# Four edits to a recurrence-and-MLP kernel: u by one row, weight sums on GpSimd, separate PSUM banks at the end, and a reordered list

## The chip, the cores and the metric

One core of a Trainium2 chip. The metric is the device time of one execution in microseconds, the median of several runs. Profiles are of one execution by the hardware profiler; its times count from the first instruction.

## The reference

Two layers run one after the other. First a recurrence over 768 steps for each of 4 sequences and 8 heads of 48 channels, with a state of 48 x 48 per head; then an MLP with the greater of two products over the 3072 tokens of width 384.

```python
for t in range(S):                                  # B, H, S, D = 4, 8, 768, 48
    kt, vt, rt, wt = (k[:, :, t], v[:, :, t], r[:, :, t], w[:, :, t])
    cur = np.einsum('bhd,bhe->bhde', u[None] * kt, vt)
    y[:, :, t] = np.einsum('bhd,bhde->bhe', rt, state + cur)
    state = wt[:, :, :, None] * state + np.einsum('bhd,bhe->bhde', kt, vt)
...
x = y.transpose(0, 2, 1, 3).reshape(B * S, H * D)   # 3072 x 384
out = np.maximum(x @ w1, x @ w2) @ w_out            # d_ff = 1024
```

All inputs and the output are float32.

## The kernel before

**Units.** The 768 steps are cut into 6 chunks of 128, the 4 sequences into 2 pairs. A unit is one chunk of one pair: 12 units, 0 to 11, with units 2c and 2c+1 being chunk c of the two pairs. Inside a unit, index b (0 or 1) is the sequence, and a tile has the 128 steps as its partitions and 8 x 48 = 384 columns.

**The recurrence of a unit** (the names are those of the list that orders the work). ScalarE takes the logarithm of w (lw; from unit 3 on also a rounded copy lwh, and VectorE the rest lwl). TensorE sums the logarithms over the steps by a product with a triangle (ex, L245), VectorE adds the step's own (incl). ScalarE makes exp of the exclusive sum (aex) and exp of minus the inclusive one (ainv), and VectorE multiplies them onto r and k (rp, kp). TensorE transposes both (T), ScalarE copies them out of PSUM (TO, tile rkT), TensorE makes the 128 x 128 products of each head (M), VectorE masks them (MO). TensorE applies them to v and, after the first chunk, adds the carried state (Y). The term with u goes another way: GpSimd multiplies k, u and r (ku L297, rku L302), VectorE sums over the 48 channels (dg), GpSimd multiplies the sum onto v (bv L310), and VectorE adds it to Y (YO). TensorE transposes the result (X), VectorE copies it (XO, tile xT). The state: K on TensorE, sa and sm on VectorE, sb on GpSimd; the chunk's decay goes through DRAM (row L268 writes the last row of incl to DRAM, wt L273 reads it back as columns into Wt, wx on ScalarE takes exp).

**The MLP of a unit.** The greater of h1 and h2 is (h1 + h2)/2 + |h1 - h2|/2. So wd = w1 - w2 and ws = w1 + w2 are built once in bfloat16 (wdif L201, wsum L198, both on VectorE), ws is transposed (wT on TensorE, wTO on ScalarE) and multiplied with w_out into wc (wp L214, 3 x 8 matmuls of 384 columns into PSUM tile wc_p; wpO on ScalarE scales by 0.5). For a unit: H (L410) makes x times wd in four groups f2 of six matmuls of 256 columns, and HO (L422) takes the absolute value on ScalarE into gT; O1 (L430) starts an output sum with three matmuls of x times wc and four of gT times w_out, O2 (L437) adds the other four; OO (L440) copies to osb on ScalarE and st (L445) stores it. O1 and O2 run for each b.

**Loads.** All go out on SP's queue, in the order of the list: ldw, ldr, ldk, ldv (L225), a whole unit (384 KB, in rows of 192 bytes) or one sequence of it (192 KB) at a time; units 0 to 2 are mostly loaded by sequence. ldw12 (L180) loads a third of w1 and of w2 (two DMAs of 512 KB), ldwo (L186) half of w_out (768 KB), which ScalarE casts to bfloat16 (woc L192). Both kinds share the same two buffers ("w12"), in turns: w12.2 takes the buffer of w12.0, wof.0 that of w12.1, wof.1 that of w12.2, when wsum and wdif have read them. u is one DMA that writes its 384 numbers to all 128 partitions (ldu L195).

**PSUM.** Tag "mlp" has two buffers and serves H, O1, wT, wp and the like; tag "ex" has two for ex and ainv.

**Order.** The list ORDER (L17) is written out by hand, and every engine works its share of it strictly in that order. A step stands as name.unit.b, or name.unit.f2 for H and HO. "warm" (L171) issues matmuls of a blank tile that nothing reads: fillers in the first 30 us, 52 in all. TensorE's order near the end of the start is

```
M.1.1 H.0.3 ex.2.0 Y.1.1 X.1.0 X.1.1 ex.2.1 H.1.0 H.1.1 K.1 wp.1 wp.0 wp.2 H.1.2 T.2.0 O1.0.0 ...
```

and ScalarE's is HO.0.2, ..., woc.0, HO.0.3, woc.1, HO.1.0, HO.1.1, aex.2.0, and on.

Of the kernel before, what the change touches and what calls it, by code (L numbers as in the profile page):

```python
# [8 lines left out]
F32 = mybir.dt.float32  # L9
# [20 lines left out]
ainv.2.1 sa.1 kp.2.1 HO.1.2 TO.2.0 ku.2.0 rku.2.0 ku.2.1 rku.2.1 sb.0.0 sb.0.1 O1.0.0 ex.3.0 incl.3.0 dg.2.0  # L30
ex.3.1 M.2.0 incl.3.1 MO.2.0 lw.4 aex.3.0 O2.0.0 O1.0.1 O2.0.1 wx.1 lwh.4 OO.0.0 vb.2.0 aex.3.1 vb.2.1 T.2.1
H.1.3 K.2 OO.0.1 O1.1.0 TO.2.1 lwl.4 sm.1 rp.3.0 dg.2.1 rp.3.1 sa.2 ainv.3.0 ainv.3.1 HO.1.3 M.2.1 Y.2.0
sb.1.0 bv.2.0 ku.3 bv.2.1 rku.3 sb.1.1 ldr.4 ldv.3 wt.2 kp.3.0 kp.3.1 MO.2.1 YO.2.0 T.3.0 TO.3.0 O2.1.0 ex.4.0
ex.4.1 incl.4.0 incl.4.1 M.3.0 Y.2.1 T.3.1 YO.2.1 O1.1.1 MO.3.0 X.2.0 X.2.1 O2.1.1 OO.1.0 lw.5 lwh.5 aex.4.0
TO.3.1 aex.4.1 rp.4.0 XO.2 M.3.1 ainv.4.0 OO.1.1 H.2.0 H.2.1 ldk.4 ldw.6 row.3 ldv.4 ldr.5 wt.3 row.4 ldk.5
vb.3 wx.2 HO.2.0 HO.2.1 K.3 rp.4.1 lwl.5 dg.3 sm.2 ainv.4.1 H.2.2 H.2.3 bv.3 ku.4 rku.4 sb.2.0 sb.2.1 kp.4.0
sa.3 kp.4.1 T.4.0 TO.4.0 HO.2.2 HO.2.3 lw.6 ex.5.0 Y.3.0 ex.5.1 T.4.1 MO.3.1 YO.3.0 M.4.0 Y.3.1 O1.2.0 O2.2.0
incl.5.0 MO.4.0 YO.3.1 incl.5.1 X.3.0 X.3.1 XO.3 TO.4.1 O1.2.1 M.4.1 O2.2.1 vb.4 aex.5.0 OO.2.0 lwh.6 rp.5.0
dg.4 lwl.6 H.3.0 Y.4.0 ainv.5.0 aex.5.1 OO.2.1 kp.5.0 rp.5.1 wx.3 HO.3.0 H.3.1 H.3.2 HO.3.1 HO.3.2 ainv.5.1
ldw.7 row.5 bv.4 sm.3 MO.4.1 kp.5.1 YO.4.0 ku.5 sb.3.0 sb.3.1 rku.5 wt.4 ldr.6 T.5.0 H.3.3 TO.5.0 HO.3.3 wx.4  # L40
lwh.7 lw.7 ex.6.0 O1.3.0 ex.6.1 incl.6.0 incl.6.1 aex.6.0 aex.6.1 Y.4.1 O2.3.0 T.5.1 YO.4.1 X.4.0 X.4.1 M.5.0
# [31 lines left out]
def kernel(  # L73
# [12 lines left out]
    nc = tc.nc  # L86
    B, H, S, D = r.shape
# [408 lines left out]
```

## Time and profile before

| | |
|---|---|
| Median of 7 runs | 160.07 us (159.03, 159.44, 159.66, 160.07, 161.06, 161.53, 161.69) |
| Profiled execution, its own time | 162.65 us |
| Its span, first to last instruction | 160.8 us |
| Busy: PE, PEld, DVE, ACT, POOL | 147.3, 100.7, 118.2, 113.7, 80.2 us |
| Mean granted TensorE clock | 0.988 |
| DMA | 28.82 MB, mean 179 GB/s; 107,802 of 112,822 packets under 512 bytes |

The span is what the profile can explain; the execution's own time is 1.85 us longer. PE is TensorE's matmuls, PEld its weight loads, DVE VectorE, ACT ScalarE, POOL GpSimd, SP the engine that issues the DMAs. A line such as L217 is a line of the kernel printed above. A row of a group gives the operation, its shapes, how often it ran, the busy time and the mean of one. A matmul's own duration overlaps the next one's, so the cost of a group of matmuls is read from the time between its starts (the chain of waits gives that). The chain of waits follows the work that ended last back from the last instruction, at each step to what released it.

### The profile page before, as it was taken

Reading aid. Unit: us, or ns where it says so; the run is one execution under the profiler, and the core shown is the slowest. Engines: PE = TensorE matmul, PEld = TensorE weight load, DVE = VectorE, ACT = ScalarE, POOL = GpSimd, SP = SyncE. Lnnn points to the kernel's source line nnn. Section 1 sums busy time; section 2 is a strip of 40 time slices with the busy share of each in tenths; the row PEclk is TensorE's granted clock in tenths of the full one; section 3 lists DMA queues with packets and bytes.
Section 4 is the critical chain, followed back from the end, with each engine's and each line's share of the span. In section 5 each row is a group of like instructions: output and inputs, shape, how many; then the busy total and the mean of one; then the engine's idle time right before and its main releaser. Section 6 shows DMA issues by size and latency. Waiting matters only on the chain.

```text
span 160.8 us, 3996 instructions
## 1 busy us (share of the span) xinstructions
PE 147.3 (92%) x1588; PEld 100.7 (63%) x1588; DVE 118.2 (73%) x185; ACT 113.7 (71%) x202; POOL 80.2 (50%) x80
## 2 busy tenths in 40 slices
PE   6988868973999999999999999979999999999991
PEld 2434434742476777768787686757786768777760
DVE  3168969871359999999799889995998888942100
ACT  4255247955789798898979889794986977664541
POOL 8274600800390862959508694890775468630000
PEclk9999999999599999999999999999999999999999
DMA  5999996996989899696999779968999994020202
GB/s 103 205 320 197 290 359 135 183 353 125 198 148 231 157 171 226 103 201 121 227 217 169 117 156 233 220 184 151 181 197 223 285 307 177 0 75 27 98 0 98
DMA packets 112822, 28.82 MB, mean 179 GB/s; under 512 B 107802, under 2 KB 112026, under 8 KB 112804
## 3 DMA queue, kind: packets, MB, share of 16 engines
q1 hardware_dynamic: 112804, 28.58, 81.7%
q8 instruction: 12, 0.20, 0.6%
q14 instruction: 6, 0.05, 0.1%
HBM read 23.82 MB, written 4.75 MB: 178 GB/s over the span
## 4 chain that ended last, share of the span: by engine, by line
PE 72%; DMA 9%; SPq 9%; DVE 3%; issue 3%; ACT 2%; DVEq 0%
PE o_p L427 20%; PE g_p L417 18%; PE o_p L433 8%; SPq L230 6%; PE tp L322 6%; DMA wof<-in_moe_w_out_dram 5%; PE mt_p L338 4%; DMA w<-in_moe_w_dram 4%; PE wc_p L217 4%; PE y_p L354 3%; PE ex_p L248 3%; PE xt_p L372 2%; PE y_p L358 2%; SPq L183 2%; PE ex_p L249 2%
## 5 line engine op out<-in xcount | busy, mean ns | idle before, releaser
L417 PE MATMUL g_p<-xT,wd_sb 128*128 128x256 bf16 x288 | 37.2, 273 | 0.6 <-ACT gT L423 0.6
L427 PE MATMUL o_p<-wo_sb,gT 128*128 128x384 bf16 x192 | 37.3, 326 | 0.0
L312 POOL TENSOR_TENSOR bv<-vt,dg 128x768 f32<-128x768 f32 (+1 forms) x15 | 20.5, 1366 | 27.3 <-DVE dg L308 13.0
L423 ACT ACTIVATE gT<-g_p 128x512 bf16<-128x512 f32 x48 | 28.0, 599 | 4.3 <-PE g_p L417 3.5
L299 POOL TENSOR_TENSOR ku<-kt,u_b 128x768 f32<-128x768 f32 (+1 forms) x15 | 22.7, 1516 | 16.5 <-DMA kt<-in_k_dram 12.8
L343 DVE TENSOR_TENSOR MTm<-mt_p,triU 128x1024 bf16<-128x1024 f32 x24 | 29.2, 1218 | 2.3 <-PE mt_p L338 2.3
L417 PEld LDWEIGHTS <-wd_sb 128*128 128x128 bf16 x288 | 26.3, 98 | 6.6 <-issue 1.6
L329 ACT COPY rkT<-tp 128x1024 bf16<-128x1024 bf16 x24 | 24.4, 1017 | 8.3 <-PE tp L322 8.3
L427 PEld LDWEIGHTS <-gT 128*128 128x128 bf16 x192 | 18.1, 98 | 11.0
L303 POOL TENSOR_TENSOR ku<-rt,ku 128x768 f32<-128x768 f32 (+1 forms) x15 | 22.4, 1494 | 2.4 <-DMA rt<-in_r_dram 1.3
L442 ACT COPY osb<-o_p 128x384 f32<-128x384 f32 x24 | 11.5, 485 | 12.0 <-PE o_p L427 11.8
L407 POOL CAST sz<-sf 48x384 bf16<-48x384 f32 x20 | 11.0, 549 | 15.5 <-DVE sf L400 14.9
L257 DVE TENSOR_TENSOR incl<-ex_p,lw 128x384 f32<-128x384 f32 x24 | 13.0, 551 | 7.2 <-PE ex_p L251 5.6
L289 DVE TENSOR_TENSOR rp<-rt,ex_p 128x384 bf16<-128x384 f32 x24 | 13.0, 548 | 5.6 <-ACT ex_p L261 5.6
L176 PE MATMUL warm<-blank,ident 128*128 128x512 bf16 x52 | 14.9, 425 | 1.5 <-POOL ident masks.py:199 1.5
L365 DVE TENSOR_TENSOR xs<-y_p,bv 128x384 bf16<-128x384 f32 x24 | 13.3, 552 | 3.6 <-PE y_p L358 3.1
L236 ACT ACTIVATE lw<-wt 128x768 f32<-128x768 f32 (+1 forms) x15 | 10.8, 722 | 7.0 <-DMA wt<-in_w_dram 7.0
L433 PE MATMUL o_p<-wc_sb,xT 128*128 128x384 bf16 x72 | 15.7, 327 | 0.0
L261 ACT ACTIVATE ex_p<-ex_p 128x384 f32<-128x384 f32 x24 | 11.5, 486 | 5.6 <-DVE incl L257 5.6
L292 DVE TENSOR_TENSOR kp<-kt,ai_p 128x384 bf16<-128x384 f32 x24 | 13.0, 548 | 2.8 <-ACT ai_p L265 2.7
L308 DVE TENSOR_REDUCE dg<-ku 128x16 f32<-128x768 f32 (+1 forms) x15 | 11.8, 785 | 0.7 <-POOL ku L303 0.7
L265 ACT ACTIVATE ai_p<-incl 128x384 f32<-128x384 f32 x24 | 12.1, 503 | 0.1
(56 smaller groups left out, 213.7 us busy)
## 6 DMA issues: line engine op xcount, KB each, us to landing
out_dram<-osb SPq DMA_DIRECT2D x24, 192.0 KB, 2.5
wt<-in_w_dram SPq DMA_DIRECT2D x9, 384.0 KB, 5.4
rt<-in_r_dram SPq DMA_DIRECT2D x9, 384.0 KB, 4.9
kt<-in_k_dram SPq DMA_DIRECT2D x9, 384.0 KB, 6.0
vt<-in_v_dram SPq DMA_DIRECT2D x9, 384.0 KB, 5.5
w<-in_moe_w_dram SPq DMA_DIRECT2D x6, 512.0 KB, 6.5
wof<-in_moe_w_out_dram SPq DMA_DIRECT2D x2, 768.0 KB
wt<-in_w_dram SPq DMA_DIRECT2D x6, 192.0 KB, 5.5
```

Of the source, the lines that this page charges most:

```text
L176: nc.tensor.matmul(x, ident, blank)
L257: nc.vector.tensor_add(flat(st["incl", i][:, b]), st["ex", i, b], flat(st["lw", i][:, b]))
L299: nc.gpsimd.tensor_mul(rows_(x), rows_(get("k", i, b)), u_b.unsqueeze(1).to_broadcast([C, x.shape[1], HD]))
L303: nc.gpsimd.tensor_mul(rows_(get("ku", i, b)), rows_(get("r", i, b)), rows_(get("ku", i, b)))
L312: nc.gpsimd.tensor_mul(x, get("v", i, b), get("dg", i, b).unsqueeze(3).to_broadcast(list(x.shape)))
L329: nc.scalar.copy(rkT, st.pop(("tp", i, b)))
L343: nc.vector.tensor_mul(x.rearrange("p a q c -> p (a q) c"), st.pop(("mt", i, b)).rearrange("p a q c -> p (a q) c"), triU.unsqueeze(1).to_b ...
L365: nc.vector.tensor_add(x, st.pop(("y", i, b)), flat(st["bv", i][:, b]))
L417: nc.tensor.matmul(g_p[:, q, :], wd_sb[:, ko, fo * C:(fo + 1) * C], st["xT", i][:, ko].rearrange("p b c -> p (b c)"), start=(ko == 0), sto ...
L423: nc.scalar.activation(st["gT", i][:, f2 * 2:f2 * 2 + 2, :], st.pop(("g", i, f2)), AF.Abs, scale=0.5)
L427: nc.tensor.matmul(st["o", i, b], st["gT", i][:, fo, b * C:(b + 1) * C], wo_sb[:, fo, :], start=False, stop=(fo == FO - 1))
L433: nc.tensor.matmul(st["o", i, b], st["xT", i][:, ko, b, :], wc_sb[:, ko, :], start=(ko == 0), stop=False)
```

## The change

- **u.** ldu writes u into one partition of its tile (1.5 KB). A product of a row of ones with it (ub, float32, PSUM tag "mlp") spreads it over 128 partitions, and ScalarE copies it back (ubO). The order on TensorE puts ub between ex.0.0 and the second group of fillers, on ScalarE ubO between ainv.0.0 and lw.0.1.
- **Weight sums.** wsum 0 to 2 and wdif 2 run on GpSimd; wdif 0 and 1 stay on VectorE. On GpSimd they stand thus: wsum.0, ku.0.0, rku.0.0, wsum.1, ku.0.1, wsum.2, rku.0.1, bv.0.0, bv.0.1, wdif.2, ku.1.0, rku.1.0, ku.1.1, rku.1.1, bv.1.0, bv.1.1.
- **The last unit's sums.** A new step O0 makes the three matmuls of x times wc with which an output sum starts; O1 calls it if it hasn't run. For unit 11 the two sums take the PSUM buffers of tag "ex", and O0.11.0 and O0.11.1 stand behind H.11.1 and H.11.3.
- **The list** is another order throughout. Among the loads, ldu comes second and ldk.0.1, ldv.0.1 come behind w12.1; row.0 and wt.0 move from in front of w_out to behind it. The two halves of w_out stand behind ldw.2.0 and ldw.2.1. The SP order from there is row.0, ldr.2.0, ldw.3, ldk.2.0, wt.0, ldr.2.1, ldw.4, row.1, ldk.2.1, ldv.2.0, ldr.3, ldk.3, ldv.2.1, where it was ldw.3, ldr.2.0, ldr.2.1, row.1, ldk.2.0, ldk.2.1, ldw.4, ldv.2.0, wt.1, ldv.2.1, ldr.3, ldk.3. H.1.0 and H.1.1 move behind the wp. There are 58 fillers.

Of the list, the start and the tail are shown.

```diff
@@ -15,57 +15,57 @@
-ldw.0.0 lw.0.0 warm_yk.8 ex.0.0 incl.0.0 aex.0.0 ainv.0.0 ldw.0.1 lw.0.1 ldr.0.0 ldk.0.0 ldv.0.0 ldu kp.0.0
-rp.0.0 warm_yk.9 T.0.0 ex.0.1 ldr.0.1 ldk.0.1 ku.0.0 rku.0.0 ku.0.1 rku.0.1 TO.0.0 incl.0.1 aex.0.1 ainv.0.1
-warm_yk.1 M.0.0 dg.0.0 rp.0.1 kp.0.1 MO.0.0 bv.0.0 ldw12.0 ldw.1.0 ldv.0.1 ldk.1.0 ldr.1.0 wdif.0 wsum.0
-warm_yk.6 T.0.1 TO.0.1 lw.1.0 warm_yk.7 ex.1.0 incl.1.0 vb.0.0 Y.0.0 M.0.1 vb.0.1 aex.1.0 ainv.1.0 ldw12.1
-row.0 ldw.1.1 ldw12.2 ku.1.0 rku.1.0 YO.0.0 dg.0.1 kp.1.0 bv.0.1 warm_tp.2 K.0 MO.0.1 rp.1.0 lw.1.1 sa.0
-wdif.1 wT.0 wTO.0 warm_tp.7 T.1.0 Y.0.1 YO.0.1 warm_mt.4 ex.1.1 X.0.0 X.0.1 wsum.1 XO.0 dg.1.0 wT.1 incl.1.1
-wsum.2 ldk.1.1 ldr.1.1 ldv.1.0 TO.1.0 wTO.1 ainv.1.1 aex.1.1 M.1.0 warm_yk.6 wT.2 wdif.2 warm_yk.2 H.0.0
-kp.1.1 rp.1.1 T.1.1 MO.1.0 vb.1.0 wTO.2 HO.0.0 H.0.1 H.0.2 Y.1.0 ldw.2.0 wt.0 ldv.1.1 ldw.2.1 TO.1.1 HO.0.1
-lw.2.0 vb.1.1 lw.2.1 wx.0 HO.0.2 M.1.1 H.0.3 ex.2.0 ldwo.0 woc.0 HO.0.3 ldwo.1 bv.1.0 ku.1.1 rku.1.1 dg.1.1
-bv.1.1 YO.1.0 MO.1.1 Y.1.1 YO.1.1 X.1.0 X.1.1 XO.1 ex.2.1 incl.2.0 H.1.0 H.1.1 incl.2.1 sm.0 ldw.3 ldr.2.0
-ldr.2.1 row.1 ldk.2.0 ldk.2.1 K.1 woc.1 HO.1.0 HO.1.1 aex.2.0 lw.3 aex.2.1 rp.2.0 rp.2.1 wp.1 wpO.1 wp.0 wp.2
-ainv.2.0 wpO.0 lwh.3 kp.2.0 lwl.3 H.1.2 T.2.0 ldw.4 ldv.2.0 wt.1 ldv.2.1 ldr.3 ldk.3 row.2 ldw.5 wpO.2
-ainv.2.1 sa.1 kp.2.1 HO.1.2 TO.2.0 ku.2.0 rku.2.0 ku.2.1 rku.2.1 sb.0.0 sb.0.1 O1.0.0 ex.3.0 incl.3.0 dg.2.0
-ex.3.1 M.2.0 incl.3.1 MO.2.0 lw.4 aex.3.0 O2.0.0 O1.0.1 O2.0.1 wx.1 lwh.4 OO.0.0 vb.2.0 aex.3.1 vb.2.1 T.2.1
...
-TO.10.1 H.9.0 H.9.1 T.11.0 M.10.1 rp.11.1 bv.10 ku.11 rku.11 sb.9.0 sb.9.1 HO.9.0 HO.9.1 MO.10.1 H.9.2 Y.10.0
-H.9.3 ainv.11.1 TO.11.0 HO.9.2 HO.9.3 YO.10.0 M.11.0 Y.10.1 kp.11.1 MO.11.0 YO.10.1 O1.9.0 T.11.1 O2.9.0
-X.10.0 X.10.1 O1.9.1 O2.9.1 vb.11 OO.9.0 dg.11 XO.10 bv.11 TO.11.1 M.11.1 OO.9.1 H.10.0 MO.11.1 Y.11.0 HO.10.0
-H.10.1 HO.10.1 H.10.2 HO.10.2 YO.11.0 Y.11.1 YO.11.1 H.10.3 O1.10.0 HO.10.3 X.11.0 O2.10.0 X.11.1 O1.10.1
-O2.10.1 OO.10.0 OO.10.1 st.5.0 st.5.1 st.6.0 st.6.1 st.7.0 XO.11 H.11.0 HO.11.0 H.11.1 HO.11.1 H.11.2 HO.11.2
-H.11.3 HO.11.3 O1.11.0 O2.11.0 O1.11.1 O2.11.1 st.7.1 st.8.0 st.8.1 st.9.0 st.9.1 st.10.0 st.10.1 OO.11.0
-st.11.0 OO.11.1 st.11.1
+ldw.0.0 ldu ldr.0.0 lw.0.0 warm_yk.9 ex.0.0 incl.0.0 aex.0.0 ldk.0.0 ainv.0.0 kp.0.0 rp.0.0 ub ubO ldw.0.1
+lw.0.1 warm_yk.9 ex.0.1 incl.0.1 aex.0.1 ldw12.0 ldr.0.1 ldw.1.0 ldv.0.0 wdif.0 ainv.0.1 rp.0.1 wsum.0 ku.0.0
+rku.0.0 vb.0.0 T.0.0 TO.0.0 warm_yk.18 M.0.0 MO.0.0 dg.0.0 ldw12.1 ldk.0.1 wdif.1 lw.1.0 ex.1.0 incl.1.0
+aex.1.0 kp.0.1 wsum.1 ku.0.1 ldw12.2 wsum.2 rku.0.1 wT.0 warm_yk.10 T.0.1 wT.1 Y.0.0 ldr.1.0 ldw.1.1 ldv.0.1
+TO.0.1 warm_mt.1 M.0.1 MO.0.1 rp.1.0 vb.0.1 lw.1.1 dg.0.1 ldk.1.0 ainv.1.0 wTO.0 wTO.1 bv.0.0 bv.0.1 YO.0.0
+kp.1.0 warm_tp.8 ex.1.1 Y.0.1 T.1.0 wdif.2 ku.1.0 rku.1.0 ldk.1.1 ldr.1.1 ku.1.1 rku.1.1 incl.1.1 YO.0.1
+ainv.1.1 wT.2 K.0 aex.1.1 TO.1.0 ldv.1.0 vb.1.0 ldv.1.1 wTO.2 vb.1.1 kp.1.1 sa.0 rp.1.1 ldw.2.0 ldwo.0 ldw.2.1
+ldwo.1 warm_mt.3 X.0.0 X.0.1 M.1.0 XO.0 T.1.1 H.0.0 MO.1.0 K.1 H.0.1 TO.1.1 lw.2.0 HO.0.0 woc.0 HO.0.1 M.1.1
+sa.1 dg.1.0 bv.1.0 MO.1.1 Y.1.0 YO.1.0 H.0.2 ex.2.0 H.0.3 Y.1.1 lw.2.1 HO.0.2 woc.1 dg.1.1 bv.1.1 YO.1.1
+ex.2.1 X.1.0 X.1.1 row.0 ldr.2.0 ldw.3 ldk.2.0 wt.0 ldr.2.1 HO.0.3 incl.2.0 aex.2.0 rp.2.0 wp.1 wpO.1 ainv.2.0
+kp.2.0 XO.1 ldw.4 row.1 ldk.2.1 ldv.2.0 ldr.3 ldk.3 ldv.2.1 wp.0 lwh.3 wpO.0 lw.3 wx.0 wp.2 wpO.2 T.2.0 H.1.0
+incl.2.1 row.2 aex.2.1 rp.2.1 TO.2.0 ainv.2.1 HO.1.0 O1.0.0 O2.0.0 ku.2.0 rku.2.0 lwl.3 sm.0 ex.3.0 incl.3.0
+kp.2.1 H.1.1 M.2.0 OO.0.0 lw.4 HO.1.1 lwh.4 sb.0.0 sb.0.1 ku.2.1 dg.2.0 bv.2.0 rku.2.1 H.1.2 ex.3.1 T.2.1
+H.1.3 MO.2.0 incl.3.1 vb.2.0 aex.3.0 HO.1.2 HO.1.3 aex.3.1 Y.2.0 lwl.4 rp.3.0 rp.3.1 TO.2.1 YO.2.0 ainv.3.0
+O1.0.1 O2.0.1 O1.1.0 M.2.1 OO.0.1 vb.2.1 ainv.3.1 kp.3.0 dg.2.1 MO.2.1 kp.3.1 T.3.0 ldw.5 TO.3.0 K.2 ex.4.0
+O2.1.0 ku.3 rku.3 bv.2.1 incl.4.0 sa.2 M.3.0 T.3.1 ex.4.1 Y.2.1 MO.3.0 YO.2.1 wt.1 ldv.3 row.3 ldr.4 ldk.4
+O1.1.1 X.2.0 X.2.1 O2.1.1 lw.5 wx.1 OO.1.0 TO.3.1 lwh.5 sm.1 incl.4.1 sb.1.0 sb.1.1 aex.4.0 OO.1.1 XO.2 M.3.1
...
+aex.11.1 HO.9.0 M.10.1 H.9.1 dg.10 ainv.11.1 HO.9.1 H.9.2 HO.9.2 T.11.0 H.9.3 kp.11.1 MO.10.1 rp.11.1 TO.11.0
+sb.9.1 bv.10 ku.11 rku.11 HO.9.3 O1.9.0 T.11.1 M.11.0 O2.9.0 YO.10.0 Y.10.1 MO.11.0 YO.10.1 dg.11 O1.9.1
+X.10.0 X.10.1 XO.10 bv.11 O2.9.1 OO.9.0 vb.11 TO.11.1 M.11.1 OO.9.1 H.10.0 MO.11.1 Y.11.0 HO.10.0 H.10.1
+H.10.2 HO.10.1 HO.10.2 YO.11.0 Y.11.1 YO.11.1 H.10.3 O1.10.0 HO.10.3 O2.10.0 X.11.0 X.11.1 OO.10.0 O1.10.1
+O2.10.1 OO.10.1 XO.11 H.11.0 H.11.1 HO.11.0 HO.11.1 O0.11.0 H.11.2 H.11.3 HO.11.2 HO.11.3 O0.11.1 st.5.1
+st.6.0 st.6.1 st.7.0 st.7.1 st.8.0 st.8.1 st.9.0 O1.11.0 O2.11.0 O1.11.1 O2.11.1 OO.11.0 OO.11.1 st.9.1
+st.10.0 st.10.1 st.11.0 st.11.1
@@ -113,6 +113,8 @@
     triR = const.tile([C, C], F32R)
     nc.gpsimd.tensor_copy(triR, triU)
     u_b = const.tile([C, HD], F32)
+    ones = const.tile([1, C], F32)
+    nc.vector.memset(ones, 1.0)
     blank = const.tile([C, 512], BF16)
     nc.vector.memset(blank, 0.0)
@@ -192,14 +194,23 @@
     def woc(half):
         nc.scalar.copy(wo_sb[:, half * FO // 2:(half + 1) * FO // 2, :], st["wof", half])
+
     def ldu():
-        nc.sync.dma_start(out=u_b, in_=u.rearrange("h d -> (h d)").unsqueeze(0).to_broadcast([C, HD]))
+        nc.sync.dma_start(out=u_b[0:1], in_=u.rearrange("h d -> (h d)").unsqueeze(0))
+
+    def ub():
+        st["ub"] = ps.tile([C, HD], F32, tag="mlp", bufs=2, name="ub_p")
+        nc.tensor.matmul(st["ub"], ones, u_b[0:1])
+
+    def ubO():
+        nc.scalar.copy(u_b, st.pop("ub"))
     def wsum(ko):
-        nc.vector.tensor_add(ws_sb[:, ko, :], st["w12", ko][:, 0, :], st["w12", ko][:, 1, :])
+        nc.gpsimd.tensor_add(ws_sb[:, ko, :], st["w12", ko][:, 0, :], st["w12", ko][:, 1, :])
     def wdif(ko):
-        nc.vector.tensor_sub(wd_sb[:, ko, :], st["w12", ko][:, 0, :], st["w12", ko][:, 1, :])
+        engine = (nc.vector, nc.vector, nc.gpsimd)[ko]
+        engine.tensor_sub(wd_sb[:, ko, :], st["w12", ko][:, 0, :], st["w12", ko][:, 1, :])
     def wT(ko):
         tp = ps.tile([C, FO, C], BF16, tag="mlp", bufs=2)
@@ -427,11 +438,19 @@
             nc.tensor.matmul(st["o", i, b], st["gT", i][:, fo, b * C:(b + 1) * C], wo_sb[:, fo, :],
                              start=False, stop=(fo == FO - 1))
-    def O1(i, b):
-        st["o", i, b] = ps.tile([C, HD], F32, tag="mlp", bufs=2, name="o_p")
+
+    def O0(i, b):
+        if i < len(units) - 1:
+            st["o", i, b] = ps.tile([C, HD], F32, tag="mlp", bufs=2, name="o_p")
+        else:
+            st["o", i, b] = ps.tile([C, HD], F32, tag="ex", bufs=2, name="ol_p")
         for ko in range(KO):
             nc.tensor.matmul(st["o", i, b], st["xT", i][:, ko, b, :], wc_sb[:, ko, :],
                              start=(ko == 0), stop=False)
+
+    def O1(i, b):
+        if ("o", i, b) not in st:
+            O0(i, b)
         out_part(i, b, 0)
     def O2(i, b):
@@ -447,11 +466,11 @@
         at = (bp * NB + b) * S + c * C
         nc.sync.dma_start(out=out[at:at + C, :], in_=st.pop(("osb", i, b)))
-    ops = dict(ldw12=ldw12, ldwo=ldwo, woc=woc, ldu=ldu, wsum=wsum, wdif=wdif, wT=wT, wTO=wTO, wp=wp, wpO=wpO,
+    ops = dict(ldw12=ldw12, ldwo=ldwo, woc=woc, ldu=ldu, ub=ub, ubO=ubO, wsum=wsum, wdif=wdif, wT=wT, wTO=wTO, wp=wp, wpO=wpO,
                ldw=ld("w", w), ldk=ld("k", k), ldr=ld("r", r), ldv=ld("v", v),
                lw=lw, lwh=lwh, lwl=lwl, ex=ex, incl=incl, aex=aex, ainv=ainv, row=row, wt=wt, wx=wx, rp=rp, kp=kp,
                ku=ku, rku=rku, dg=dg, bv=bv, vb=vb, T=T, TO=TO, M=M, MO=MO, Y=Y, YO=YO, X=X, XO=XO,
-               K=K, sa=sa, sm=sm, sb=sb, H=Hf, HO=HO, O1=O1, O2=O2, OO=OO, st=out_st, **{f"warm_{t}": warm(t) for t in ('mt', 'tp', 'yk')})
+               K=K, sa=sa, sm=sm, sb=sb, H=Hf, HO=HO, O0=O0, O1=O1, O2=O2, OO=OO, st=out_st, **{f"warm_{t}": warm(t) for t in ('mt', 'tp', 'yk')})
     with tc.manual_schedule():
         for step in ORDER.split():
             name, *at = step.split(".")
```

## The prediction

> **What bounds the kernel now.** I read the slices first, then the chain of waits, then the windows of the first 44 us.
>
> The slices of the profiled execution (40 of 4.02 us):
>
> ```profile
> PE   6988868973999999999999999979999999999991
> DVE  3168969871359999999799889995998888942100
> PEclk9999999999599999999999999999999999999999
> DMA  5999996996989899696999779968999994020202
> ```
>
> TensorE is full from the eleventh slice (40 us) to the last. Before that it has holes, and part of its 147.3 us is filler (the warm group of the page: 52 matmuls, 14.9 us). The DMA engines are near full from the second slice on. So the first 40 us must be settled by something else than TensorE, and the chain says by what:
>
> ```profile
> 15.18 6.44 DMA w<-in_moe_w_dram
> ...
> 29.67 8.73 DMA wof<-in_moe_w_out_dram
> 38.43 1.47 ACT wo_sb L193
> 39.90 0.51 ACT gT L423
> 40.45 5.74 PE wc_p L217 x24
> ...
> 157.41 0.48 ACT osb L442
> ```
>
> Until 38.43 the chain is loads and their issue on SP. The second half of w_out (wof.1) lands at 38.4, ScalarE casts it (woc.1), one gT eviction frees the PSUM buffer, and the products wc_p start at 40.45. From there the chain is TensorE almost without a break to 157.4, and the last eviction and store end it. So what counts is when wc_p can start, and how much TensorE work is left then: 160.8 - 40.45 = 120.35 us now.
>
> Windows of that start (columns: stretch, length, busy time and count of PE, PEld, DVE, ACT, POOL, granted clock, DMA share, GB/s):
>
> ```profile
> 2.00:6.00 4.00, 4.00 (x10) 1.59 (x9) 0.21 (x1) 0.54 (x2) 3.09 (x6) 1.00 1.07 214
> 14.00:18.00 4.00, 3.08 (x45) 1.72 (x43) 3.98 (x6) 2.21 (x5) 1.15 (x1) 1.00 0.84 177
> 24.00:26.00 2.00, 1.68 (x24) 1.06 (x22) 2.00 (x5) 1.53 (x2) 0.00 (x0) 1.00 0.56 110
> 37.00:39.00 2.00, 1.05 (x22) 0.79 (x21) 0.00 (x0) 0.57 (x1) 0.00 (x0) 1.00 0.22 44
> 37.45:40.85 3.40, 1.00 (x22) 0.69 (x20) 0.00 (x0) 2.42 (x4) 0.00 (x0) 1.00 0.61 119
> 40.90:44.28 3.38, 3.38 (x13) 1.61 (x11) 1.66 (x3) 2.37 (x5) 1.41 (x2) 0.50 1.04 199
> ```
>
> Loads of 192-byte rows move at about 204 GB/s with the DMA engines full (4 to 8 us), so a half of r, k, v or w (196.6 KB) costs 0.96 us; the long rows of w_out move at 353 GB/s (32 to 36 us). Three stretches are thin: 14 to 18 loses 0.64 us of DMA time, 24 to 26 loses 0.88, 26 to 30 (share 0.89) 0.44: 1.96 together. 37 to 39 loses another 1.56. In the last line TensorE has half its clock just as wc_p runs: its 24 matmuls take 5.74 us where the same shape takes 0.163 a piece later (8 in 1.30), 3.91 in all: 1.8 us are lost.
>
> **The change, part by part.** The sum is made against the profiled execution: span 160.8, with what lies around it 162.65. That is 2.6 above the median of the runs, 160.07; the 1.8 of the half clock would explain most of it. I carry differences over to the median.
>
> *u as one row.* The broadcast (192 KB in 1.5 KB rows) leaves the stream in front of w_out; 1.5 KB takes its place. At the 353 GB/s of such rows it costs 0.56, at the rate of the 192-byte loads 0.96; [...] I take 0.9. Added: a product of float32, 384 columns (nearest row: ex_p L251, 0.8 to 0.9 us for one) ahead of the second fillers, which give that time back, and a copy on ScalarE (0.485, the row of L442) before 10 us, where ScalarE is idle more than half the time. Both cost nothing as long as the load covers them; uncovered, 1.4.
>
> *row.0 and Wt.0 move behind w_out.* They are three issues on SP (0.30 and 1.10 us) and about 0.4 us of DMA time for 4-byte pieces, at 15.7 and 26.2. They stand in or beside two thin stretches. Bounds for what of the 1.96 lost there goes: 0 and 1.96. The cause isn't shown, the place fits: I take two thirds, 1.3.
>
> *The rest of the loads.* All 16 halves of units 0 and 1, the six loads of w1 and w2 and the two w halves of unit 2 still stand ahead of wof.1, in another order. Together: woc.1 starts at 38.43 - 0.9 - 0.4 - 1.3 = 35.8. wof.0 has one w half less ahead: its cast starts at 34.85 - 0.96 - 2.6 = 31.3.
>
> *wc_p.* H.1.0 and H.1.1 move behind it, so no gT eviction stands between woc.1 and wc_p: it starts at 35.8 + 1.47 + 0.05 = 37.3, 3.1 earlier. The 12 matmuls moved are 12 x 0.109 = 1.3 us more behind it. Net 1.8.
>
> *Weight sums on GpSimd.* VectorE loses three of 1.216 and one of 1.223 (L199, L202): 4.9 us that nothing waited for on the path. On GpSimd no such form stands in the trace; nearest are the products of L299, 1.018 for 384 columns and 1.847 for 768, so 2.16 ns a column and 2.4 us for 1024 (upper end; the line of bv, 0.866 and 1.699, gives 2.25). Queued behind them: ku and rku of units 0 and 1, bv, and through the buffers the loads w12.2, wof.0, wof.1. Walk: w12.2 has landed by about 19; wsum.2 to 21.4, rku.0.1 to 22.4, bv.0.0 and bv.0.1 to 24.6 (the second half of v.0 is now late, at about 22.5), wdif.2 to 27.0, four ku and rku of 1.0 to 31.0, bv.1.1 by 32.8. X.1, which stands ahead of wc_p on TensorE, needs it 0.9 before 37.3: 3.6 us are spare. wof.1 needs the buffer at 27.0; its data would move only after wof.0 and a w half, past 32. Also covered.
>
> [...] The trace:
>
> ```profile
> 45.89 1.00 POOL L303 TENSOR_TENSOR ku<-rt,ku 128x384 f32<-128x384 f32 x1
> 46.18 1.53 DVE L243 TENSOR_TENSOR lwl<-lw,lwh 128x768 fp32r<-128x768 f32 x1 [1.89 <-ACT lwh L240]
> 51.34 0.95 DVE L243 TENSOR_TENSOR lwl<-lw,lwh 128x768 fp32r<-128x768 f32 x1
> ```
>
> The first lwl took 0.58 longer; waiting for the end of ku would have cost 0.71. [...] by the row 2.0. Both give 0 on the path.
>
> *The list after wc_p.* Behind wof.1 came w.3, r.2, k.2, w.4 and v.2; now r.3 and k.3 (3.9 us) stand ahead of the last half of v.2 too. Before, that half was issued at 45.60, and v takes at least 3.1 us to land: 48.7. After: 48.7 - 2.6 - 0.4 (Wt.1 moved behind) + 3.9 = 49.6, cast by 50.1. TensorE reaches K.2, the first that needs it, 14.8 us after wc_p begins (3.9 + three transposes 1.35 + H.1 2.6 + o_p 4.75 + two ex_p 1.0 + two M 0.66 + Y 0.5), at 52.1: 2.0 spare. T.2.0 at 41.2 needs k.2.0 (39.1, with kp 39.7). What the other permutations do inside TensorE's full stretch can't be read; it has 1.3 us of visible holes in 40 to 120, so I take 0, with -1 and +1.
>
> *The tail.* O0 puts six matmuls between the H.11 and lets them not wait for an eviction. The H.11 now take 2.88 for 24 x 0.109 = 2.62, and the next group 0.60 for 0.49: at most 0.37; I take 0.3. The end (0.48, the store) stays.
>
> *The clock.* [...] The trace shows it after 3.40 us with 1.00 us busy, [...]; by the row it may: ahead of wc_p stand Y, ex and X, about 1.4 busy of 3.4. Nearer to the row: I take no difference.
>
> Sum: -3.1 + 1.3 - 0.3 = -2.1. Span 158.7, execution 160.5, median 160.07 - 2.1 = 158.0.
>
> **The rivals.**
> - *All the thin DMA time goes, or the half clock does:* another 0.7 to 1.56 from the loads, or up to 1.8. For: the places fit. Against: nothing in the change touches 37 to 39. 155.4 to 157.0.
> - *The gain is hidden anyway:* [...] only u's 0.9 and the eviction's 0.5 remain, less 1.3. For: 1.56 us are lost just there. 159.3 to 160.7; that is also the case where the edits do nothing that shows.
> - *Slower: v.2's last half holds TensorE at K.2.* Place: TensorE's queue in order. Price: each us beyond the 2.0 spare costs one; it ends behind the old kernel once the half is 4.1 late, over 1% behind at 5.7. For: 3.9 us of loads put ahead, thin stretches of 1 to 2 us, Wt.0 waiting on SP for row.0 to land. Against: the half was ready 3 us ahead so far (cast at 51.86, and only ScalarE's order held it). 161 to 163.
>
> **How the numbers follow.** The likeliest 0.57, its own range 157.0 to 159.2; the greater gain 0.18; hidden 0.15; slower 0.10. A measurement of this kernel tells about 1% (158.5 and 161.7) from no change. Faster by over 1%: 0.43 of the likeliest and all of the greater gain, 0.61. Within 1%: 0.14 of the likeliest, 0.15, and 0.01 of the slower: 0.30. Slower: 0.09. Leaving out the lower half of the second case and nearly all of the last, the range is 156.0 to 160.8.
>
> **What would show it.** woc.1 starting at 35 to 36.5 and wc_p directly behind it; GpSimd's sums at 2.2 to 2.6; bv.1.1 before 35; K.2 without a wait for v; DMA share above 0.9 in 14 to 30. Wrong if wc_p starts after 39, if TensorE shows a wait for DMA or GpSimd between 37 and 60, or if the stretch from the start of wc_p to the end is not 121.4 (120.35 + 1.3 - 0.3) within 2 us.

## The result, and the profile after

157.55 us, median of 12 runs (157.05 to 158.18), against 160.18 for the kernel before in the runs beside them: ratio 0.985, 95% interval 0.982 to 0.988, so 2.4 us less. Ratios, here and below, leave out executions in a slower state, so they need not be the quotient of the medians (these are 2.6 apart). Predicted: 158.0. The profiled execution took 157.31, its span 155.5; that is 5.3 below the span shown of before, 160.8, because that profiled execution of before was one of the longer ones (162.65 against its median of about 160).

The slices of the kernel after, 40 of 3.89 us:

```profile
PE   6999766989999999999999999999999999999991
DVE  3163826994599999899999997979997897782100
PEclk9999999999999999999999999999999999999999
DMA  4998988999999895999979999967769899020202
```

In this profile TensorE is full from the tenth slice instead of the eleventh, the one slice of half clock is gone, and so is the 7 of PE at slice 27 (104 to 109 us). VectorE's 118.2 us of busy time are now 113.9, GpSimd's 80.2 are 89.9.

The chain of waits of the kernel after (start, length, what):

```profile
10.93 3.37 POOL ws_sb L209
...
17.46 5.76 DMA vt<-in_v_dram
...
32.90 1.36 ACT wo_sb L195
34.26 0.51 ACT gT L434
...
36.56 0.48 PE xt_p L383 x6
37.04 3.90 PE wc_p L228 x24
...
152.11 0.48 ACT osb L461
```

In before the chain hung on the load wof.1 until 38.43. Now no load of w_out is in it. The last load in it is the second half of v.0, issued at 17.46; after that come ScalarE's copies and casts in their order (in the 3.4 us from 32.6 to 36.0 ScalarE is busy for 3.40), then X.1, then wc_p. A new link near its start is the weight sum on GpSimd, 10.93 to 14.30. The second ainv of unit 1 on ScalarE (ainv.1.1), the second cast (woc.1) and the products wc_p:

```profile
27.53 0.49 ACT L276 ACTIVATE ai_p<-incl 128x384 f32<-128x384 f32 x1 [1.12 <-DVE incl L268]
35.60 1.47 ACT L195 CAST wo_sb<-wof 128x1536 bf16<-128x1536 f32 x1
36.88 4.06 PE L228 MATMUL wc_p<-wo_sb,wsT_sb 128*128 128x384 bf16 x24
```

Windows of the start, to be set beside those of before (length, then busy time and count of PE, PEld, DVE, ACT, POOL, granted clock, DMA share, GB/s):

```profile
12.00:14.00 2.00, 2.00 (x11) 0.93 (x10) 0.54 (x2) 1.07 (x2) 2.00 (x1) 1.00 0.73 208
14.00:18.00 4.00, 3.98 (x31) 1.98 (x29) 2.30 (x3) 0.78 (x2) 2.73 (x4) 1.00 1.05 371
24.00:26.00 2.00, 1.17 (x4) 0.40 (x3) 0.78 (x3) 2.00 (x4) 2.00 (x4) 1.00 0.79 153
37.00:39.00 2.00, 2.00 (x15) 1.18 (x13) 0.55 (x1) 1.58 (x5) 0.00 (x0) 1.00 0.68 120
```

The thin stretches of before are filled or half filled (14 to 18: 0.84 to 1.05; 24 to 26: 0.56 to 0.79; 37 to 39: 0.22 to 0.68). A new one stands at 12 to 14 us, 0.73 where before had 1.10.

### The profile page after: what moved, and what is told of

It is laid out like the page before. It is cut to its first block, busy times and chain, and to the rows that moved or that the text cites. A ratio compares the mean times of both kernels' runs of the same rounds, so it can differ in the third digit from the quotient of the medians.

```text
span 155.5 us, 4021 instructions
## 1 busy us (share of the span) xinstructions
PE 146.6 (94%) x1596; PEld 101.7 (65%) x1596; DVE 113.9 (73%) x182; ACT 113.8 (73%) x203; POOL 89.9 (58%) x84
## 4 chain that ended last, share of the span: by engine, by line
PE 75%; DMA 7%; ACT 7%; SPq 5%; POOL 2%; issue 1%; DVE 1%; POOLq 0%; ACTq 0%
PE g_p L428 20%; PE o_p L438 19%; PE o_p L448 7%; PE tp L333 6%; PE mt_p L349 4%; DMA vt<-in_v_dram 4%; DMA w<-in_moe_w_dram 4%; SPq L241 3%; PE y_p L365 3%; PE xt_p L383 3%; PE ex_p L259 3%; PE wc_p L228 3%; PE y_p L369 2%; POOL ws_sb L209 2%; PE ex_p L260 2%; PE kv_p L396 2%
## 5 line engine op out<-in xcount | busy, mean ns | idle before, releaser
L438 PE MATMUL o_p<-wo_sb,gT 128*128 128x384 bf16 x176 | 34.2, 326 | 0.0
L434 ACT ACTIVATE gT<-g_p 128x512 bf16<-128x512 f32 x48 | 28.6, 600 | 5.2 <-PE g_p L428 4.3
L323 POOL TENSOR_TENSOR bv<-vt,dg 128x768 f32<-128x768 f32 (+1 forms) x15 | 19.4, 1299 | 8.2 <-DVE dg L319 4.2
L461 ACT COPY osb<-o_p 128x384 f32<-128x384 f32 x22 | 10.6, 482 | 10.3 <-PE o_p L438 10.2
L178 PE MATMUL warm<-blank,ident 128*128 128x512 bf16 x58 | 15.6, 419 | 1.5 <-POOL ident masks.py:199 1.5
L448 PE MATMUL o_p<-wc_sb,xT 128*128 128x384 bf16 x66 | 14.4, 327 | 0.0
L326 ACT CAST vb<-vt 128x768 bf16<-128x768 f32 (+1 forms) x15 | 10.6, 709 | 4.0 <-DMA vt<-in_v_dram 4.0
L209 POOL TENSOR_TENSOR ws_sb<-w 128x1024 bf16<-128x1024 f32 x3 | 9.1, 3045 | 7.0 <-DMA w<-in_moe_w_dram 7.0
```

The source lines that it names most:

```text
L178: nc.tensor.matmul(x, ident, blank)
L323: nc.gpsimd.tensor_mul(x, get("v", i, b), get("dg", i, b).unsqueeze(3).to_broadcast(list(x.shape)))
L434: nc.scalar.activation(st["gT", i][:, f2 * 2:f2 * 2 + 2, :], st.pop(("g", i, f2)), AF.Abs, scale=0.5)
L438: nc.tensor.matmul(st["o", i, b], st["gT", i][:, fo, b * C:(b + 1) * C], wo_sb[:, fo, :], start=False, stop=(fo == FO - 1))
L448: nc.tensor.matmul(st["o", i, b], st["xT", i][:, ko, b, :], wc_sb[:, ko, :], start=(ko == 0), stop=False)
```

## The experiments

All were timed against the kernel before on the same chip, in three sets of four, each set on one chip. Beside the three sets the kernel before took 158.93, 159.17 and 159.06. My theory after the result: loads and ScalarE's order decide when wc_p starts, the stretch from there to the end is nearly fixed, so each part is worth what it moves that start, plus the tail. The rival: the gain is the clock, which the kernel before loses and the new one doesn't. In the first four expectations the letters A, B and C are theories of that experiment alone. From the fifth on they are: A, u's 192 KB early in the stream cost the most; B, the tail's banks do; C, the first weight sum on GpSimd costs a microsecond; D, it doesn't show at the end.

**Edits without the list**

```diff
-... ldv.0.0 ldu kp.0.0 ...          HO.11.1 H.11.2 ... HO.11.3 O1.11.0
+... ldv.0.0 ldu ub ubO kp.0.0 ...   HO.11.1 O0.11.0 H.11.2 ... HO.11.3 O0.11.1 O1.11.0
```
(with the changed functions, otherwise the old list)

> The old list with the three edits in it (u by one row and a product, weight sums on GpSimd, O0 in its own banks), nothing else moved. Theory A (the loads ahead of w_out bind the start, so u's 0.9 us counts in any order, and the tail gives 0.3): 1.2 us faster than before, woc.1's cast of the second half of w_out starts about 0.9 earlier. Theory B (the list made the gain, the edits alone are hidden behind the thin DMA stretches): within 0.3 of before.

Measured: 158.41, ratio 0.9962 (0.9939 to 0.9985). That is 0.6 us, half of what A said and twice the limit of B. The cast woc.1 starts at 36.03.

**The list without the edits**

```diff
-ub ubO O0.11.0 O0.11.1     (the new list without these four)
```

> The new list without the three edits: u broadcast by DMA in second place, all weight sums on VectorE, the last sums in the shared banks. Theory A: loses u's 0.9 and the tail's 0.3 against the changed kernel, so about 1.3 us faster than before and the cast of the second half of w_out at 36.5. Theory B: nearly all of the gain, 2.2 to 2.6 us faster than before.

Measured: 158.45, ratio 0.9969 (0.9943 to 0.9995). That is 0.5 us, less than either theory said; woc.1 starts at 35.38. Edits and list give 1.1 apart and 2.4 together.

**A filler against the half clock, in the old list**

```diff
-K.1 woc.1 HO.1.0
+K.1 warm_mt.10 woc.1 HO.1.0
```

> The old kernel with ten more filler matmuls of 512 columns (2.2 us at full clock) in TensorE's hole between K.1 and wc_p, where nothing else can run. Theory A (the idle stretch ahead of wc_p costs the clock): no half clock between 40 and 45 us, wc_p in 3.9 us where it took 5.74, median 0.5 to 1.0 us lower (some executions had no half clock before), the highest times gone. Theory B (the half clock comes from elsewhere or its cost is hidden): within 0.3 of before, or 0 to 0.3 slower if the fillers delay wc_p.

Measured: 159.53, ratio 1.0023 (1.0002 to 1.0044). On that chip 9 of the 55 runs of the kernel before had a mean clock of 0.979 to 0.989, and they are the ones of 159.95 to 162.76; of the 22 with the filler none was under 0.996. So the half clock makes before's long executions, the profiled one among them, and not its median: with it gone the rest pays about half a microsecond for the filler. The clock as the source of the gain falls by the changed kernel too: 5 of its 12 executions have a mean clock of 0.985 to 0.989 (median 157.81; 157.18 for the other seven), so it does not avoid the half clock. The profile of the filler version is also the cleanest view of the old order (TensorE, start, length):

```profile
36.43 2.33 PE L175 MATMUL warm<-blank,ident 128*128 128x512 bf16 x10
38.60 0.65 PE L216 MATMUL wc_p<-wo_sb,wsT_sb 128*128 128x384 bf16 x3
```

wof.1 was cast at 35.45 here, not at 38.43, and from wc_p to the end it is 118.54 us, not 120.40.

**All weight sums on VectorE, in the changed kernel**

```diff
-        nc.gpsimd.tensor_add(ws_sb...
+        nc.vector.tensor_add(ws_sb...
-        engine = (nc.vector, nc.vector, nc.gpsimd)[ko]
+        engine = nc.vector
```

> The changed kernel with all four weight sums of GpSimd back on VectorE, list as changed. Theory A (off the path on both engines): within 0.3 of the changed kernel, 157.3 to 157.9; GpSimd reaches the last bv of unit 1 two to three us earlier. Theory B (VectorE's 4.9 us of sums stand in front of what unit 0 and 1 need): 0.5 to 1.5 slower than the changed kernel. Theory C (the collisions of the two engines' sums, 1.0 us twice in its trace, and the load of the last third of w1 and w2 that waits for the first sum, do cost): 0.3 to 0.8 faster than the changed kernel.

Measured: 156.54, ratio 0.9846 (0.9815 to 0.9877), the same as the changed kernel (A). Moving the sums earns nothing.

**u by broadcast again, in the changed kernel**

```diff
-        nc.sync.dma_start(out=u_b[0:1], in_=u.rearrange("h d -> (h d)").unsqueeze(0))
+        nc.sync.dma_start(out=u_b, in_=u.rearrange("h d -> (h d)").unsqueeze(0).to_broadcast([C, HD]))
```
(and without ub and ubO)

> The changed kernel with u's broadcast load put back at the same place of the list, and the product with ones and its copy left out. Theory A (u's 192 KB stand second in the load stream, so every load behind them comes later, and in the new list nothing else absorbs it): the cast woc.1 starts 0.9 to 1.9 us later than in the changed kernel, wc_p with it, and 1.0 to 1.9 of the 2.4 us gained are lost: ratio to the kernel before 0.991 to 0.997. Rival B (it is the tail's banks that make the list pay): the time stays within 0.4 us of the changed kernel, ratio 0.983 to 0.988. The prediction's own term: 0.9 us, ratio 0.991.

Measured: 157.73, ratio 0.9895 (0.9848 to 0.9942): 0.7 us worse than the changed kernel; the cast woc.1 starts at 36.3 against 35.6, wc_p at 37.35 against 36.88. That is near the prediction's term of 0.9 and below A's range; B's lies below it, and the interval reaches into both.

**Without the last unit's own banks**

```diff
-        if i < len(units) - 1:
+        if True:
```
(and without O0.11.0 and O0.11.1 in the list)

> The changed kernel with the last unit's output sums back in the mlp buffers and without the steps O0 (their matmuls start with O1). The prediction: 0.3 us worse than the changed kernel, ratio 0.987. Theory A: 0 to 0.4 worse, and the loss is in the last 8 us alone. Rival B: 1 to 1.9 us worse, ratio 0.991 to 0.997.

Measured: 157.11, ratio 0.986 (0.9821 to 0.9899): 0.15 us worse, B falls. The traces give the size more exactly than the times. The last matmuls of this kernel:

```profile
145.52 3.04 PE L427 MATMUL g_p<-xT,wd_sb 128*128 128x256 bf16 x24
148.52 0.65 PE L447 MATMUL o_p<-wc_sb,xT 128*128 128x384 bf16 x3
149.01 1.46 PE L437 MATMUL o_p<-wo_sb,gT 128*128 128x384 bf16 x8
150.31 0.65 PE L447 MATMUL o_p<-wc_sb,xT 128*128 128x384 bf16 x3
```

and those of the changed kernel, from the run beside the last three experiments:

```profile
145.32 1.54 PE L428 MATMUL g_p<-xT,wd_sb 128*128 128x256 bf16 x12
146.70 0.65 PE L448 MATMUL ol_p<-wc_sb,xT 128*128 128x384 bf16 x3
147.19 1.47 PE L428 MATMUL g_p<-xT,wd_sb 128*128 128x256 bf16 x12
148.50 0.65 PE L448 MATMUL ol_p<-wc_sb,xT 128*128 128x384 bf16 x3
```

From the first H.11 to the end of TensorE's work it is 6.74 us in all seven profiles without the edit and 6.43 in all seven with it: 0.31.

**row.0 and Wt.0 behind w_out, in the old list**

```diff
-ldw12.1 row.0 ldw.1.1 ... ldw.2.0 wt.0 ldv.1.1 ... wx.0 ... ldwo.1 ... ldr.2.0 ldr.2.1
+ldw12.1 ldw.1.1 ... ldw.2.0 ldv.1.1 ... ldwo.1 row.0 ... ldr.2.0 wt.0 ldr.2.1 ... wx.0
```
(sm.0, which needs them, further back)

> The kernel before with the decay's way through DRAM moved behind w_out alone: row.0 behind the second half of w_out, Wt.0 behind r.2, exp and the state's product with it further back. The prediction's terms: 0.4 of DMA time and two thirds of 1.96 us of thin stretches go, so woc.1 starts up to 1.7 earlier: ratio 0.990. Rival (the thin stretches are made by something else, [...]): woc.1 within 0.5 us of where it was, ratio 0.997 to 1.002.

Measured: 158.58, ratio 0.9964 (0.9937 to 0.9991), 0.6 us, less than half of the prediction's terms. Its woc.1 starts at 35.09, in the filler version at 35.45. Two of its windows:

```profile
14.00:18.00 4.00, 3.43 (x48) 1.95 (x46) 3.98 (x6) 2.46 (x6) 1.21 (x3) 1.00 1.05 236
24.00:26.00 2.00, 1.63 (x13) 0.61 (x10) 1.38 (x3) 1.78 (x3) 0.00 (x0) 1.00 0.38 76
```

The stretch at 14 to 18 is full, but it is so in the filler version too (1.07), which leaves row.0 where it was; the one at 24 to 26 is thinner than ever without Wt.0 (0.38). So these steps didn't make the thin stretches.

**u by one row alone, in the old list**

```diff
-ldu kp.0.0
+ldu ub ubO kp.0.0
```

> The kernel before with u as one row alone: product with ones and copy in front of kp.0.0, list otherwise the old one. The prediction's term: 0.9 us off the loads, wc_p 0.9 earlier, ratio 0.994. Theory A in the old list, where u's load stands eighth: 0.4 to 0.9 gained, ratio 0.994 to 0.998, about all of what the three edits together gave there (0.996). Rival: nothing, ratio 0.999 to 1.001, since in the old list wof.1 waits for the buffer of w12.2 and for issue slots and not for u's bytes.

Measured: 159.25, ratio 0.9993 (0.9968 to 1.0019): nothing. The profile says why. VectorE, then TensorE of this kernel:

```profile
52.20 1.02 DVE L300 TENSOR_TENSOR kp<-kt,ai_p 128x384 bf16<-128x384 f32 x2 [1.02 <-DMA kt<-in_k_dram]
...
49.13 0.43 PE L393 MATMUL kv_p<-vb,kp 128*64 128x48 bf16 x16
...
52.81 0.40 PE L330 MATMUL tp<-ident,kp 128*128 128x128 bf16 x4 [0.82 <-DVE kp L300]
```

and TensorE of the filler version, where wc_p starts 0.55 later (38.60 against 38.05):

```profile
49.51 0.43 PE L384 MATMUL kv_p<-vb,kp 128*64 128x48 bf16 x16
...
52.05 0.39 PE L321 MATMUL tp<-ident,kp 128*128 128x128 bf16 x4
```

wc_p starts earlier, and then T.3.0, the transposes of unit 3, waits for the load k.3: from K.2 (kv_p) to the transposes of kp it is 3.68 us instead of 2.54. Its place in the list is the old one, and SP issued it no earlier: at 45.37, against 44.39 in the filler version.

**The changed kernel and three versions on one chip**

```diff
 (no edit)
```

> The changed kernel itself, beside the three that follow on the same chip, since it was measured on another chip than the version with all weight sums on VectorE. Both theories: ratio to the kernel before 0.985, within 0.004.

Measured: 157.16, ratio 0.9846 (0.9801 to 0.9892).

All weight sums on VectorE, the edit as above:

> The changed kernel with all weight sums on VectorE, measured beside the changed kernel. Theory C (the sum of the first third on GpSimd, held up by VectorE's difference, frees the buffer 1.2 us later, so the load w12.2 is issued later and all behind it): faster than the changed kernel by 0.8 to 1.6 us, as in the profiles (wc_p at 35.3 against 36.9); ratio 0.975 to 0.980. Theory D (as the two separate measurements said, 0.9846 and 0.985: a start won there is lost again before the end): within 0.4 us of it, ratio 0.983 to 0.987.

Measured: 156.40, ratio 0.9842 (0.9779 to 0.9906).

The new list with u as one row, and nothing else:

```diff
-ub ubO kp... O0.11.0 ... O0.11.1      (the new list; ub, ubO and the one-row load kept, O0 left out)
```

> The kernel before with the new list and u as one row; weight sums on VectorE, the last unit's sums in the mlp buffers. Theory A (u's 192 KB stand second in the stream): 0.7 to 1.2 us faster than the list alone (0.9969), so 0.990 to 0.992; what is left to the version with the tail's banks as well (0.9846) is then 0.9 or more. Rival (the list and u's row together make the whole gain, the tail next to nothing): 0.984 to 0.987, wc_p at 35.0 to 35.6.

Measured: 157.49, ratio 0.9916 (0.9883 to 0.9949). 0.8 us better than the list alone: A's size.

```diff
-        nc.gpsimd.tensor_add(ws_sb[:, ko, :], ...
+        engine = (nc.vector, nc.gpsimd, nc.gpsimd)[ko]
+        engine.tensor_add(ws_sb[:, ko, :], ...
```

> The changed kernel with the sum of the first third of w1 and w2 alone back on VectorE. Theory C: the load w12.2 is issued 1.0 to 1.5 us earlier and the kernel ends 0.8 to 1.5 us earlier than the changed kernel, as with all sums on VectorE or a little better, because GpSimd keeps the other three off VectorE: ratio 0.974 to 0.980. Theory D: within 0.4 us of the changed kernel.

Measured: 156.75, ratio 0.984 (0.9782 to 0.9898).

The cost that C names is seen at the start. What SP waited for between 5 and 20 us, the changed kernel first, then the one with all sums on VectorE:

```profile
SPq L185 <- POOL ws_sb L209: 1.9, 1, 1.9
```

```profile
SPq L185 <- DVE ws_sb L209: 1.5, 1, 1.5
```

The load w12.2 is issued at 14.31 and 13.94 in the two profiles of the changed kernel, at 13.13 and 13.58 with VectorE, at 13.16 with the first sum alone put back; wc_p starts at 36.88 and 36.56, at 35.31 and 35.90, and at 35.70. At the end the medians differ by 0.8 and 0.4 us in the same direction, the ratios by 0.0004 and 0.0006, with intervals of half a per cent each way. The half clock blurs this comparison: two of the six executions with all sums on VectorE met it (mean clock 0.986 and 0.989) and took 158.28 and 158.29, the other four 156.07 to 156.43; the three of the changed kernel at full clock took 156.41 to 157.34. Between C and D it stays open; that the sums on GpSimd gain nothing is certain, and no version is shown to be better than the changed kernel.

What all profiles show together (us):

| version | wc_p starts | from there to the end |
|---|---|---|
| before | 40.45 | 120.40 |
| old list, the three edits | 38.18 | 118.65 |
| old list, filler | 38.60 | 118.54 |
| old list, u alone | 38.05 | 119.95 |
| old list, row.0 behind | 37.11 | 119.58 |
| new list alone; with u | 36.75; 36.31 | 118.97; 118.96 |
| changed, without the tail's banks | 36.76 | 118.95 |
| changed, u by broadcast | 37.35 | 118.64 |
| changed (two profiles) | 36.88; 36.56 | 118.66; 118.65 |
| changed, sums on VectorE (two) | 35.31; 35.90 | 118.65; 118.66 |
| changed, first sum alone on VectorE | 35.70 | 118.65 |

In the new list the second column, but for the tail's 0.31, doesn't depend on the first: whatever the start gains, the end gains. In the old list (the tail's 0.31 set aside) an earlier start is partly or wholly taken back. I hold this for the source of the 1.3 us by which the whole is more than its parts. The half clock is not: executions with a mean clock of 0.995 or more alone give 0.2 and 0.9 apart (158.64 and 157.95 against 158.86) and 2.4 together (156.58, three executions, against 158.98). At T.3.0 the loss is shown (1.14 of the 1.41 that u alone loses against the filler version); that r.3 and k.3 further ahead cure it was not tried alone, nor was H.1 behind the wp. And the difference between the list with u (0.9916) and the same with the tail's banks (0.9846, 0.9842) is larger than the tail's 0.31; the rest lies ahead of wc_p (36.31 against 35.31 and 35.90), where the two kernels are the same, and stays open.

## Why the prediction was right, point by point

- *What bounds the kernel.* Right: the start of wc_p and a fixed stretch behind it. But two things of that profile belong to one execution: wof.1 cast at 38.43 (35.1 to 36.0 in the four other profiles with the old list) and the half clock. I carried "38.43 minus" over to the median; the median of before fits wc_p at about 38.7 (an estimate: 159.06 less 1.8 around the span, less 118.54; no profile shows before itself without the half clock). And the last wait is no longer the load of w_out, as I had it, but ScalarE's own order: in eight of the nine profiles with the new list wc_p starts 9.34 or 9.35 us after ainv.1.1 (27.53 to 36.88 in the one shown), in the ninth, the list with u, 9.56.
- *woc.1 at 35.8.* It started at 35.6 and 35.2. That the number fits is in part luck: by the estimate of 38.7 the cast stood at about 36.7 (less 0.55 and 1.47) and moved by 1.1 to 1.5, not by 2.6 from 38.43. Of the three terms, u's 0.9 measures 0.7 to 0.8 in the new list and nothing alone in the old one; row.0 and Wt.0 with the thin stretches, 1.7, measure 0.6 in time, and the thin stretches weren't theirs.
- *wof.0 at 31.3.* 32.8 and 32.5: w12.2's issue waits for the weight sum on SP, which I walked on GpSimd but not on SP, and the chain of the profile shown leads from there through v.0 to ScalarE; with all sums on VectorE it is 31.2 and 31.8.
- *wc_p at 37.3, straight behind the cast.* 36.9 and 36.6, before the cast ends (37.07 in the first): the first four products read the first half of w_out only. All profiles with the new list show wc_p ahead of that end. In the old list it came 0.55 behind the cast, for the gT eviction.
- *Weight sums.* GpSimd and VectorE in the kernel after:

```profile
10.90 3.38 POOL L209 TENSOR_TENSOR ws_sb<-w 128x1024 bf16<-128x1024 f32 x1 [5.81 <-DMA w<-in_moe_w_dram]
21.82 2.36 POOL L209 TENSOR_TENSOR ws_sb<-w 128x1024 bf16<-128x1024 f32 x1
35.02 0.83 POOL L323 TENSOR_TENSOR bv<-vt,dg 128x384 f32<-128x384 f32 x1 [1.13 <-DVE dg L319]
```

```profile
10.85 1.23 DVE L213 TENSOR_TENSOR wd_sb<-w 128x1024 bf16<-128x1024 f32 x1
17.47 1.23 DVE L213 TENSOR_TENSOR wd_sb<-w 128x1024 bf16<-128x1024 f32 x1 [0.56 <-DMA w<-in_moe_w_dram]
```

  2.36 us alone (estimate 2.4). Two of the four start beside a difference on VectorE and take 3.38 and 3.39: 1.02 and 1.03 more, where the difference ran on for 1.18 and 1.19 us. The differences took 1.23 each. That is 2.0 us on GpSimd's walk, the figure taken from the row of lwl; what delays the sum is not shown. bv.1.1 ran at 35.02, not at 32.8, and X.1 followed at 36.56: the 3.6 us of cover were all but used up. But it was not the queue of sums that used them: GpSimd stood idle for 1.13 in front of bv.1.1, waiting for VectorE's dg, and with all sums on VectorE bv.1.1 stands as close ahead of wc_p (33.33 and 35.31, against 35.02 and 36.88).

  In the profile from the last runs the second pair started the other way round, and VectorE was the one that took longer (GpSimd, VectorE, TensorE):

```profile
16.35 2.34 POOL L209 TENSOR_TENSOR ws_sb<-w 128x1024 bf16<-128x1024 f32 x1 [0.40 <-DMA w<-in_moe_w_dram]
16.45 3.33 DVE L213 TENSOR_TENSOR wd_sb<-w 128x1024 bf16<-128x1024 f32 x1
20.76 0.40 PE L333 MATMUL tp<-ident,kp 128*128 128x128 bf16 x4 [2.45 <-DVE kp L303]
```

  VectorE's difference took 2.1 us more than its 1.23 (GpSimd's sum had 2.24 left), kp.0.1 behind it came late, and TensorE stood still for 2.45. The chain of waits of that profile runs through the difference, so the 0 on the path failed there: I had taken it as covered. Cost at the end: between nothing and 0.8.
- *The list after wc_p.* v.2's last half, predicted cast by 50.1, and K.2, predicted at 52.1:

```profile
50.85 0.51 ACT L326 CAST vb<-vt 128x384 bf16<-128x384 f32 x1 [0.65 <-DMA vt<-in_v_dram]
```

```profile
51.55 0.43 PE L396 MATMUL kv_p<-vb,kp 128*64 128x48 bf16 x16
```

  It was ready 0.2 us ahead, not 2.0; the slower rival was near and didn't come, by luck more than by my sum. What I priced as a risk alone, r.3 and k.3 ahead of it, goes with a T.3.0 that no longer waits: TensorE shows no wait between 37 and 60 us.
- *The stretch, 121.4.* Measured 118.66, 2.7 less, outside my 2 us: by that sign the prediction was wrong here. Its terms: the tail 0.31, as predicted; the 12 moved matmuls 1.3, kept as predicted and not measured alone; the half clock 1.86 (120.40 less 118.54), which I had left in; and a hole of 0.86 in the old list (in all five of its profiles) that the new one lacks, where I took 0 with -1 and +1. Before, and the list alone from 100 to 110 us:

```profile
107.62 0.44 PE L248 MATMUL ex_p<-lwh,triR 128*128 128x384 f32 x1 [0.86 <-DVE rp L289]
```

```profile
100.00:110.00 10.00, 10.00 (x129) 7.41 (x126) 9.00 (x17) 9.09 (x17) 9.70 (x7) 1.00 0.69 139
```

  118.54 + 1.3 - 0.86 - 0.31 = 118.67. So the part behind wc_p gives nothing (+0.1), and the gain is in the start: 38.7 (estimate) to 36.6 or 36.9.
- *The sum.* 2.1 predicted, 2.4 measured (1.9 by the medians of the last runs). The mechanism holds in outline (an earlier wc_p, a nearly fixed stretch behind it, a small gain at the tail). That the sum fits is luck in part: the term of the thin stretches and row.0 was 1.1 too large, and the hole with the first products that need no second half, together about 1.1, stood against it.

## What to carry to other kernels

Before a wait of one profile is priced, ask whether it belongs to the kernel or to that execution; the profiles of the variants of one list show it at once. A start that comes earlier is worth only what the next load in the queue allows, so an edit can be worth nothing in one order of loads and its full size in another (u by one row: ratio 0.9993 in the old list, 0.8 us in the new one). A sum moved to an idle engine is costed on the queue that waits for its buffer too (here w12.2 was issued at 14.31 and 13.94, against 13.13 and 13.58), and on the engine whose work beside it can take longer (2.1 us of VectorE here).

## What the runs showed of the hardware

In three of the fourteen profiles the granted clock was halved before the end: those of before, of the version without the tail's banks and of the changed kernel from the last runs (mean clock 0.988 each, the other eleven 0.996 to 1.000). Each time it followed a stretch in which TensorE was little busy but not idle. In before that was 1.00 us of 3.40 (37.45 to 40.85), and the clock was 0.50 from 40.90 to 44.28. In the changed kernel:

```profile
18.41:21.81 3.40, 1.04 (x20) 0.96 (x21) 2.29 (x3) 1.09 (x2) 3.40 (x3) 1.00 1.07 213
21.81:25.22 3.41, 2.96 (x14) 1.24 (x15) 2.31 (x4) 3.41 (x6) 2.95 (x4) 0.50 0.79 156
```

The version without the tail's banks, and then the three edits in the old list, show one window each:

```profile
18.76:22.17 3.41, 1.04 (x20) 0.96 (x21) 1.97 (x3) 1.43 (x2) 3.41 (x2) 1.00 1.17 220
26.29:29.70 3.41, 1.81 (x18) 1.26 (x19) 1.92 (x3) 1.62 (x3) 3.41 (x3) 1.00 1.01 163
```

The half clock followed the first of these two windows and not the second (mean clock 0.988 and 0.997). In the first profile of the changed kernel (mean clock 1.000) TensorE was busy for 1.41 us of the 3.40 from 18.30 to 21.70, and no half clock followed. So one kernel met the half clock in one execution and not in the other; what sets it off is not shown.

In the profile from the last runs the thin window is made by a wait: it holds most of TensorE's 2.45 us for kp, behind the difference that took 3.33 us beside GpSimd's sum. That this wait brought the half clock on was not tried.

What the half clock cost differed. In before it fell on wc_p, whose 24 matmuls took 5.74 us on the chain, against 3.90 in the kernel after. In the profile from the last runs it fell at 21.81 to 25.22, ahead of wc_p, which still starts at 36.56, against 36.88 in the other profile of the changed kernel. Over the executions (median with a mean clock under 0.99, against the others) it is 2.6 us in the kernel before (161.46 against 158.86), 1.5 in the new list alone (159.46 against 157.95), 0.6 in the changed kernel (157.81 against 157.18) and none that shows with the three edits in the old list (158.34 against 158.64).
